# Moving the layer-norm statistics of blocks 8 to 15 into the kernel-generation stage, and splitting two first Fourier stages into halves, in a one-core S4D-plus-GLU kernel

## The chip, the cores and the metric

The kernel runs on one core of a Trainium2 chip. The metric is the device time of one execution in microseconds. The core's engines are PE (TensorE, matrix multiplies; PEld is its weight load), DVE (VectorE), ACT (ScalarE), POOL (GpSimd) and SP (SyncE, which here only issues DMA transfers). Each engine works through its own instructions in order. DMA transfers are issued from queues on SP, ACT and POOL and carried out by sixteen DMA engines.

## The reference

The input u is one sequence of 2048 tokens with 448 features, all in fp32. It is normalised once, and two branches are computed from the normalised sequence and added to u.

```python
xn = layernorm(u)                                  # per token, over 448 features
# branch A: a diagonal state-space convolution, one kernel K of 2048 taps per feature
dt = exp(log_dt); A = -exp(log_A_real) + 1j * A_imag
C  = (C_real + 1j * C_imag) * dt
K  = 2 * real(sum_n C[d, n] * exp(A[d, n] * dt * l))          # 448 x 256 states x 2048 taps
a  = irfft(rfft(xn, 4096) * rfft(K, 4096), 4096)[:2048] + xn * D_skip
# branch B: a gated linear unit with 1792 hidden features
b  = (sigmoid(xn @ w_gate) * (xn @ w_up)) @ w_down
out = u + a + b
```

## The kernel before

**Blocks.** The 2048 tokens are 16 blocks of 128. A block's normalisation needs two statistics per token (mean and variance), from which `x_scales` works out the scale `ys` and the shift `zs` by three Newton steps on DVE. `x_stats` (L246) is one BN_STATS (L248) and one BN_AGGR (L249) of a block; `x_scales` (L251 to L263) is a dozen tiny DVE instructions for as many blocks as one call names; `x_load` (L242) fetches a group of blocks by four DMAs, one for every 32 partitions.

**Two programs, interleaved.** `conv()` is branch A and `glu()` is branch B. Both are Python generators; a loop at the end of the kernel always advances the one that has done the smaller share of its total, where each `yield` states how much work lies behind it. A tile framework then places the instructions on the engines, guided by priorities (`hp`) and by `issue_after`, which holds an instruction back until another one has been issued.

`conv()` goes through these stages:
- startup: it loads blocks 0 to 7 (acc), some weights and the state-space parameters, then blocks 8 to 15 into two tiles (xe0 and xe1, L1037), normalises and transposes the first blocks (L270, L212), and works out the parameters (`prep`, mostly DVE: L300 to L414). After blocks 0 to 7 the statistics of blocks 8 to 15 are taken (L1063 to L1066). The space of xe0 and xe1 is then used for other tiles, P0/P1 and x1a/x1b. The phases go to DRAM (ph_d).
- `kgen` (from L445): 56 chunks, each building a part of the convolution kernel's spectrum. For a chunk, SP loads phases (ph, L475), PE selects them (tr, L526), ACT takes sines of them (S, L535 to L538), POOL multiplies magnitudes (me and mf, L491 and L503), DVE multiplies both (Et at L589 and L590, Ft at L591), and PE contracts Et with Ft (ko, L603). Each fourth chunk is followed by a first Fourier stage of what was gathered (kp and kq, L553), whose result goes through a tile sk to DRAM.
- `spectra`: the products of the spectra and the way back (sp L891, pv L918, L953).

`glu()` runs the 14 tiles of 128 hidden features twice, once for blocks 0 to 7 (half 0) and once for blocks 8 to 15 (half 1). Fp32 products are made of three products of high and low parts. Per tile and group of 512 tokens there are two groups of eleven gate matmuls (gu, L696), a tanh (th, L704), the product hf (L707), its high and low parts hh and hl (L712, L714), and then the down product (po, L809), added up by DVE in acc (L814). In half 0 each tile's weights are loaded (wraw L629 and L631, rd L637), split (wh L746, wl L750, dh and dl) and, for most tiles, also stored in DRAM (wt_d L753, dt_d L776).

**The cross stage.** The last group of half 0 (tiles 12 and 13) also prepares blocks 8 to 15, in pairs of blocks 8, 10, 12 and 14 (a pair is named by its first block): `pair_load` fetches a pair, `pair_norm` normalises it (L270 and L272), `pair_turn` transposes it (L212), and `pair_first` does its first Fourier stage: eight small matmuls (L281) into four PSUM banks named gu, four ACT copies (L678) and eight DMA stores from ACT's queue (L680). Three short tables say where these steps stand: `mid` (between the two gate groups of a tile and token group), `end` (behind it) and `downs` (in the down products). The pool of gu banks has four, shared by gate groups, po, kq, transposes and `pair_first`.

The tables of the kernel before are

```python
mid = [(pair_norm, 8), None, (pair_first, 8), (pair_first, 10)]
end = [(), ((pair_turn, 8), (pair_norm, 10)), ((pair_turn, 10), (pair_norm, 12)), ((pair_turn, 12), (pair_norm, 14))]
downs = {(0, 0): (pair_first, 12), (0, 1): (pair_turn, 14), (0, 3): (pair_first, 14)}
```

## Time and profile before

| what | value |
|---|---|
| median of three runs | 748.35 us (746.88 to 749.01) |
| the profiled execution | 751.69 us |
| its span, first to last instruction | 749.9 us |
| mean granted TensorE clock | 0.981 |
| PE busy | 701.9 us, 94% |
| DVE busy | 558.9 us, 75% |
| ACT and POOL busy | 425.6 us (57%) and 348.2 us (46%) |

The profiled execution has its own time, 751.69 us; its span is 1.8 us shorter, since something lies around the first and last instruction. Durations are read from that execution. A row such as `L603 PE MATMUL ko<-Et,Ft ... [1.54 <-DVE Et L589]` is an instruction of line 603 on PE that writes tile ko from tiles Et and Ft, and before which PE was idle for 1.54 us until DVE's Et of line 589 was there. "x12" stands for twelve in a row. The granted clock is the share of TensorE's full speed that the chip allowed in that stretch.

### The profile page before, as it was taken

The numbers are of one execution on the slowest core, as the hardware profiler recorded it, in microseconds if no ns is written. First come the engines' busy times: TensorE is split into PE (matmuls) and PEld (weight loads), VectorE is DVE, ScalarE is ACT, GpSimd is POOL, SyncE is SP. The second block draws the span as 40 slices with busy tenths as digits, with TensorE's granted clock in tenths as the row PEclk, the third lists the DMA queues.
The fourth block names the chain that finished last, engine by engine and source line by source line (L and its number), as shares of the span: only waits on it lengthen the run. The fifth ranks groups of instructions, "written<-read, shape, count | busy, mean of one in ns | idle before, by whom it ended". The sixth has DMA issues, their size and how long they took to land.

```text
span 749.9 us, 19404 instructions
## 1 busy us (share of the span) xinstructions
PE 701.9 (94%) x7892; PEld 551.8 (74%) x7892; DVE 558.9 (75%) x776; ACT 425.6 (57%) x651; POOL 348.2 (46%) x423
## 2 busy tenths in 40 slices
PE   3997988999999899899999999999999999998995
PEld 2765766887877687666788887887877777776784
DVE  5889996689979789868677978877974555555533
ACT  3553853588677868797676787687743222313320
POOL 2110064785956855846554586387755001351002
PEclk9999998999999999999999999999999999999998
DMA  9965347253225443456942331232158999999845
GB/s 206 232 183 145 87 129 220 62 188 127 72 67 165 127 135 92 136 178 163 278 132 68 109 92 67 91 97 68 42 159 229 268 239 238 236 282 232 198 120 161
DMA packets 98952, 114.75 MB, mean 153 GB/s; under 512 B 11888, under 2 KB 86832, under 8 KB 98864
## 3 DMA queue, kind: packets, MB, share of 16 engines
q1 hardware_dynamic: 74704, 89.11, 43.8%
q10 hardware_dynamic: 21584, 18.24, 8.9%
q0 software_dynamic: 2576, 6.17, 3.2%
q8 instruction: 62, 1.02, 0.6%
q14 instruction: 26, 0.21, 0.1%
HBM read 69.64 MB, written 43.84 MB: 151 GB/s over the span
## 4 chain that ended last, share of the span: by engine, by line
PE 64%; DVE 11%; DMA 8%; ACT 5%; POOL 4%; issue 3%; SPq 3%; ACTq 0%; DVEq 0%; POOLq 0%
PE gu L696 23%; PE po L809 14%; PE sp L891 7%; PE tr L526 7%; PE ko L603 6%; PE pv L918 4%; POOL me L503 2%; PE kp L553 1%; DVE Ft L591 1%; DMA xe<-in_A_u_dram 1%; POOL mf L503 1%; DMA sx<-x_d 1%; DMA ph<-ph_d 1%; DMA wraw<-in_B_w_gate_dram 1%; DVE wl L750 1%
## 5 line engine op out<-in xcount | busy, mean ns | idle before, releaser
L503 POOL TENSOR_TENSOR me<-me,pm 128x32 f32<-128x32 f32 (+1 forms) x168 | 135.1, 804 | 136.2 <-DVE Et L590 125.5
L503 POOL TENSOR_TENSOR mf<-mf,pm 128x64 f32<-128x64 f32 (+1 forms) x112 | 107.4, 959 | 4.6
L696 PE MATMUL gu<-xh,wh 128*128 128x512 f32 x336 | 100.3, 405 | 5.2 <-DVE hf L707 3.4
L696 PE MATMUL gu<-xh,wl 128*128 128x512 f32 x336 | 96.8, 395 | 0.0
L696 PE MATMUL gu<-xl,wh 128*128 128x512 f32 x336 | 96.6, 393 | 0.0
L589 DVE TENSOR_TENSOR Et<-me,S 128x1024 f32<-128x1024 f32 x56 | 80.1, 1430 | 17.1 <-ACT S L538 16.8
L590 DVE TENSOR_TENSOR Et<-me,S 128x1024 f32<-128x1024 f32 x56 | 76.4, 1364 | 16.5 <-ACT me L516 10.7
L809 PE MATMUL po<-dh,hh 128*128 128x448 f32 x224 | 84.9, 380 | 3.9 <-DVE acc L814 3.3
L809 PE MATMUL po<-dl,hh 128*128 128x448 f32 x224 | 82.6, 369 | 0.0
L809 PE MATMUL po<-dh,hl 128*128 128x448 f32 x224 | 82.3, 369 | 0.1
L591 DVE TENSOR_TENSOR Ft<-mf,S 128x1024 f32<-128x1024 f32 x56 | 77.7, 1387 | 3.3 <-ACT S L538 3.1
L696 PEld LDWEIGHTS gu<-xh,wh 128*128 128x128 f32 x336 | 61.2, 190 | 25.7 <-issue 4.7
L535 ACT ACTIVATE S<-tr 128x1024 f32<-128x1024 f32 x56 | 57.5, 1027 | 35.7 <-PE tr L526 35.5
L707 DVE SCALAR_TENSOR_TENSOR hf<-th,gu 128x512 f32<-128x512 f32 x56 | 38.2, 682 | 49.6 <-PE gu L696 38.4
L696 PEld LDWEIGHTS gu<-xh,wl 128*128 128x128 f32 x336 | 63.9, 190 | 14.3 <-DVE wl L750 0.3
L603 PEld LDWEIGHTS ko<-Et,Ft 128*32 128x32 f32 x3584 | 53.7, 110 | 28.0 <-issue 12.7
L696 PEld LDWEIGHTS gu<-xl,wh 128*128 128x128 f32 x336 | 63.5, 189 | 13.7
L603 PE MATMUL ko<-Et,Ft 128*32 128x64 f32 x3584 | 63.9, 221 | 9.4 <-DVE Ft L591 7.8
L712 ACT CAST hh<-hf 128x512 fp32r<-128x512 f32 x56 | 34.9, 623 | 60.8 <-DVE hf L707 58.3
L526 PE MATMUL tr<-sel,ph 128*128 128x512 f32 x224 | 66.5, 419 | 0.4 <-ACT sk L559 0.2
L704 ACT ACTIVATE th<-gu 128x512 f32<-128x512 f32 x56 | 33.7, 601 | 58.4 <-PE gu L696 45.6
L538 ACT ACTIVATE S<-S,hpi 128x1024 f32<-128x1024 f32 x56 | 65.3, 1165 | 0.0
(199 smaller groups left out, 1321.5 us busy)
## 6 DMA issues: line engine op xcount, KB each, us to landing
sk_d<-sk ACTq DMA_DIRECT2D x14, 512.0 KB
sx<-x_d SPq DMA_DIRECT2D x32, 224.0 KB
skl<-sk_d SPq DMA_DIRECT2D x16, 448.0 KB
vp<-v_d SPq DMA_DIRECT2D x16, 448.0 KB
v_d<-vt SPq DMA_DIRECT2D x62, 112.0 KB
wt_d<-wh SPq DMA_DIRECT2D x9, 512.0 KB
wt_d<-wl SPq DMA_DIRECT2D x9, 512.0 KB
wl<-wt_d SPq DMA_DIRECT2D x9, 512.0 KB
```

The lines of the kernel that those rows point to most:

```text
L503: ins = nc.gpsimd.tensor_tensor(m[:, :, w + a : 2 * w : n], m[:, :, a:w:n], par(base + i).unsqueeze(2).to_broadcast([128, 4 * DC, w // n]) ...
L526: nc.tensor.matmul(ps[:, h], ph[:, cn % 2, 128 * h : 128 * h + 128], sel[:, i], start=(i == 0), stop=(i == 1),)
L535: nc.scalar.activation(rows(cs), pv, AF.Abs)
L538: sins[:] = [nc.scalar.activation(cs, cs, AF.Sin, scale=-TWO_PI, bias=hpi)]
L589: v.tensor_tensor(Et[:, :, :, 32:64], two(me[:, :, 32:64]), S[:, 1::-1], ALU.mult)
L590: v.tensor_tensor(Et[:, :, :, 0:32], two(me[:, :, 0:32]), S[:, 1:3, :, ::-1], ALU.mult)
L591: fts[:] = [v.tensor_tensor(Ft, two(mf), S[:, 3:5], ALU.mult)]
L603: mm = nc.tensor.matmul(ko[32 * j : 32 * j + 32, sl], Ft[:, cc, DC * h + 4 * q + j], Et[:, cc, DC * h + 4 * q + j], start=(k == 0), stop=( ...
L696: glu_mm[:] = [nc.tensor.matmul(ps, a_, b_, start=(n == 0), stop=(n == len(mm) - 1))]
L707: marks[1] = v.scalar_tensor_tensor(hf, th, 1.0, pgu[1], ALU.add, ALU.mult)
L809: glu_mm[:] = [nc.tensor.matmul(po, a_[:, bs], w_, start=(n == 0), stop=(n == 3 * fc - 1))]
L891: mm = nc.tensor.matmul(to, tb[:kk, t, 64 * c : 64 * c + 64], rhs, start=True, stop=True, skip_group_check=True,)
```

## The change

It has two parts.

The statistics of blocks 8 to 15 are no longer taken in the startup. The two tiles xe0 and xe1 and their eight loads go; P0/P1 and x1a/x1b get tiles of their own, of the same sizes. Instead, in `kgen`, at the place of the former `yield 34` ahead of the first chunk, four rounds each load a pair of blocks (four DMAs of 32 x 896) into the first part of tile sk and take its statistics, with a yield of 34/4 behind each; the scales of all eight blocks are worked out at the end. All four rounds use the same buffer, so that a round's loads wait until DVE has read the round before.

`pair_first` is generalised to `pair_part(b, xns, gs)`, which does only the groups gs. For the pairs 8 and 10 groups 0 and 1 (`pair_low`, two banks) stay at the place of `pair_first`, and groups 2 and 3 (`pair_high`) move to the end of the third and the fourth step of the cross stage. The pairs 12 and 14 keep all four groups in one place.

```diff
@@ kgen
-        yield 34
+
+        xe = tl["sk"].rearrange("p k e -> p (k e)")[:, : 2 * D].rearrange("p (b d) -> p b d", b=2)
+        for b in range(8, 16, 2):
+            x_load(xe, b, 2, [nc.sync])
+            for i in range(2):
+                x_stats(sm, b + i, xe[:, i])
+            yield 34 / 4
+        x_scales(sm, 8, 8)
@@ pair_first
-    def pair_first(b, xns):
+    def pair_part(b, xns, gs):
-        x1 = pg.tile([128, 2, D], F32, name="x1", tag="wraw", bufs=1)
-        pss = [psg.tile([128, 512], F32, name="gu", bufs=4) for _ in range(4)]
-        for g in range(4):
-            x_first_stage(pss[g][:, :D], xns, g)
-        for g in range(4):
+        x1 = pg.tile([128, 2, D], F32, name="x1", tag="wraw", bufs=1) if 0 in gs else None
+        pss = [psg.tile([128, 512], F32, name="gu", bufs=4) for _ in gs]
+        for ps, g in zip(pss, gs):
+            x_first_stage(ps[:, :D], xns, g)
+        for ps, g in zip(pss, gs):
             to = x1[:, g] if g < 2 else pg.tile([128, D], F32, name="x1", tag="rd", bufs=RB)
-            nc.scalar.copy(to, pss[g][:, :D])
+            nc.scalar.copy(to, ps[:, :D])
             for i in range(2):
                 nc.scalar.dma_start(x1_d[:, row(b + i, g)], to[64 * i : 64 * i + 64])
+    pair_first, pair_low, pair_high = (functools.partial(pair_part, gs=gs) for gs in (range(4), (0, 1), (2, 3)))
@@ glu, cross
-                    mid = [(pair_norm, 8), None, (pair_first, 8), (pair_first, 10)]
-                    end = [(), ((pair_turn, 8), (pair_norm, 10)), ((pair_turn, 10), (pair_norm, 12)), ((pair_turn, 12), (pair_norm, 14))]
+                    mid = [(pair_norm, 8), None, (pair_low, 8), (pair_low, 10)]
+                    end = [(), ((pair_turn, 8), (pair_norm, 10)), ((pair_turn, 10), (pair_norm, 12), (pair_high, 8)), ((pair_turn, 12), (pair_norm, 14), (pair_high, 10))]
@@ conv, startup
-("P2", [CP, 2, 2 * N], F32R), ("xe0", [128, 2048], F32), ("xn0", [128, 4, D], F32), ("xe1", [128, 4, D], F32),
+("P2", [CP, 2, 2 * N], F32R), ("p01", [CP, 2, 2, 2 * N], F32R), ("xn0", [128, 4, D], F32), ("x1ab", [128, 2, 2, D], F32),
-                for q in range(2):
-                    x_load(xes[q], 8 + 4 * q, 4, [nc.sync])
-                with tc.issue_after(xls[0].ins):
-                    for b in range(8):
-                        x_stats(sm, 8 + b, xes[b // 4][:, b % 4])
-                x_scales(sm, 8, 8)
```

The lines of the changed kernel stand seven further down from L573 on, and ten further down behind `pair_part`, so that L589, L603, L696 and L707 of before are its L596, L610, L706 and L717.

The order in which the framework places the instructions changes at three places. The first is DVE's startup, between the Fourier copies of the first blocks (xr, L225) and the parameter work. Before, it read

```order
L225 TENSOR_TENSOR xr<-gu,xr 64x512
L248 BN_STATS st_84<-xe_116 128x6 x4
L300 TENSOR_SCALAR ex<-ex,lim 112x514 x2
L707 SCALAR_TENSOR_TENSOR hf<-th,gu 128x512
L248 BN_STATS st_84<-xe_118 128x6 x4
L249 BN_AGGR mv<-st_84 128x2 x5
L714 TENSOR_TENSOR hl<-hf,hh 128x512
L249 BN_AGGR mv<-st_84 128x2 x3
L750 TENSOR_TENSOR wl<-wraw,wh 128x1024
L707 SCALAR_TENSOR_TENSOR hf<-th,gu 128x512
L256 TENSOR_SCALAR ve<-mv 128x8
```

and now it reads

```order
L225 TENSOR_TENSOR xr<-gu,xr 64x512
L300 TENSOR_SCALAR ex<-ex,lim 112x514 x2
L717 SCALAR_TENSOR_TENSOR hf<-th,gu 128x512
L724 TENSOR_TENSOR hl<-hf,hh 128x512
L717 SCALAR_TENSOR_TENSOR hf<-th,gu 128x512
L760 TENSOR_TENSOR wl<-wraw,wh 128x1024
L724 TENSOR_TENSOR hl<-hf,hh 128x512
L717 SCALAR_TENSOR_TENSOR hf<-th,gu 128x512
L306 SCALAR_TENSOR_TENSOR fr<-ki,ex 112x514 x2
```

All statistics are gone from there, and L306 of the parameter work follows the third hf. On DVE the statistics now stand among the first chunks of `kgen`; the second to the fourth round read

```order
L598 TENSOR_TENSOR Ft<-mf_1054,S_1053 128x1024
L248 BN_STATS st_84<-sk 128x6 x2
L824 SCALAR_TENSOR_TENSOR acc<-po,acc 128x448
L249 BN_AGGR mv<-st_84 128x2 x2
L717 SCALAR_TENSOR_TENSOR hf<-th,gu 128x512
L724 TENSOR_TENSOR hl<-hf,hh 128x512
L248 BN_STATS st_84<-sk 128x6 x2
L249 BN_AGGR mv<-st_84 128x2 x2
L596 TENSOR_TENSOR Et_1050<-me_1055,S_1049 128x32x32
L597 TENSOR_TENSOR Et_1050<-me_1055,S_1049 128x32x32
L598 TENSOR_TENSOR Ft<-mf_1054,S_1049 128x1024
L248 BN_STATS st_84<-sk 128x6 x2
```

The first Ft here belongs to the first chunk, the second Ft to the second, and behind the last BN_STATS come an hf, a wl and the scales, mixed with the Et and Ft of the next chunks.

The second place is SP's queue at the first phase loads. Before, it held

```order
L475 DMA ph_1095<-ph_d 8x2x256 x6
L475 DMA ph_1096<-ph_d 8x2x256 x6
L753 DMA wt_d<-wh 128x1024
L753 DMA wt_d<-wl 128x1024
L629 DMA wraw<-in_B_w_gate_dram 128x3x128
L631 DMA wraw<-in_B_w_gate_dram 64x128 x2
L629 DMA wraw<-in_B_w_up_dram 128x3x128
L631 DMA wraw<-in_B_w_up_dram 64x128 x2
L776 DMA dt_d<-dh 128x448
L776 DMA dt_d<-dl 128x448
L637 DMA rd<-in_B_w_down_dram 128x448
L475 DMA ph_1095<-ph_d 8x2x256 x6
```

and from the first wraw on it now holds (with two sk loads ahead of the first ph and two ahead of wt_d)

```order
L636 DMA wraw<-in_B_w_gate_dram 128x3x128
L638 DMA wraw<-in_B_w_gate_dram 64x128 x2
L244 DMA sk<-in_A_u_dram 32x896 x4
L636 DMA wraw<-in_B_w_up_dram 128x3x128
L638 DMA wraw<-in_B_w_up_dram 64x128 x2
L244 DMA sk<-in_A_u_dram 32x896 x4
L786 DMA dt_d<-dh 128x448
L786 DMA dt_d<-dl 128x448
L475 DMA ph_1057<-ph_d 8x2x256 x4
L244 DMA sk<-in_A_u_dram 32x896 x4
L475 DMA ph_1057<-ph_d 8x2x256 x2
```

Each group of four sk loads of these rows waits for DVE's statistics of the round before; the last stands between the fourth and the fifth of six phase loads.

The third place is PE's order at the first `pair_first` of the cross stage. Before, it read

```order
L526 MATMUL tr<-sel,ph_1096 128x512 x4
L281 MATMUL gu<-xt,wx 64x448 x6
L603 MATMUL ko<-Et_1089,Ft 32x64 x32
L281 MATMUL gu<-xt,wx 64x448 x2
L696 MATMUL gu<-xh,wh 128x512 x3
L696 MATMUL gu<-xr,wh 128x512
L696 MATMUL gu<-xh,wl 128x512 x3
L696 MATMUL gu<-xr,wl 128x512
L696 MATMUL gu<-xl,wh 128x512 x3
L553 MATMUL kp<-wk,ks 64x64 x5
```

and now it reads

```order
L526 MATMUL tr<-sel,ph_1058 128x512 x4
L281 MATMUL gu<-xt,wx 64x448 x4
L706 MATMUL gu<-xh,wh 128x512 x3
L706 MATMUL gu<-xr,wh 128x512
L706 MATMUL gu<-xh,wl 128x512 x3
L706 MATMUL gu<-xr,wl 128x512
L706 MATMUL gu<-xl,wh 128x512 x3
L553 MATMUL kp<-wk,ks 64x64 x7
L610 MATMUL ko<-Et_1051,Ft 32x64 x32
```

The gate group of eleven moved ahead of the chunk's ko, and half of the eight L281 stands later, around the next chunk's ko. Between 165 us and the cross stage, and behind it, the engines' orders are the same before and after but for a few neighbouring loads.

11 lines of the change are left out of this document (4 added, 7 removed).

## The prediction

> **What bounds the kernel now.** I began with the head of the page and its busy line.
>
> ```profile
> span 749.9 us, 19404 instructions
> PE 701.9 (94%) x7892; PEld 551.8 (74%) x7892; DVE 558.9 (75%) x776; ACT 425.6 (57%) x651; POOL 348.2 (46%) x423
> ```
>
> PE is the bound on average, so an engine that is not PE matters only where PE waits for it. Next I asked for the busy time by stretches, because 94% is an average over stages. The columns are the stretch, its length, then busy time (and instructions) of PE, weight load, DVE, ACT and POOL, then granted clock, share of the DMA engines and GB/s.
>
> ```profile
> 28.00:41.30 13.30, 13.30 (x63) 10.10 (x62) 10.25 (x25) 8.79 (x15) 1.13 (x1) 1.00 0.90 196
> 41.30:55.00 13.70, 13.70 (x67) 9.47 (x66) 13.53 (x33) 5.91 (x10) 1.86 (x1) 1.00 0.64 189
> 55.00:112.00 57.00, 49.87 (x237) 36.98 (x236) 56.42 (x87) 32.42 (x53) 13.26 (x7) 0.97 0.43 122
> 131.00:165.00 34.00, 33.98 (x329) 28.06 (x329) 24.55 (x25) 22.95 (x32) 27.39 (x33) 1.00 0.34 109
> 152.00:165.00 13.00, 12.98 (x176) 10.37 (x175) 10.58 (x9) 10.27 (x15) 10.63 (x11) 1.00 0.53 173
> 165.00:187.00 22.00, 20.91 (x229) 17.13 (x227) 20.13 (x27) 17.59 (x26) 13.00 (x15) 1.00 0.44 148
> 600.00:680.00 80.00, 76.98 (x626) 58.86 (x626) 43.37 (x85) 21.31 (x42) 20.40 (x25) 1.00 1.07 253
> ```
>
> Three things are to be seen. From 55 to 112 us DVE is busy 56.42 of 57 us and PE only 49.87: there DVE sets the pace, and DVE work taken away ahead of it should come straight off the time. From 131 to 165 PE is full and DVE has 34 − 24.55 = 9.45 us free. From 600 to 680 the DMA engines are full; that stage's transfers follow from what is computed before them, so I take it to move as a block with what lies ahead.
>
> The chain of waits shows what the startup hangs on (start, duration, what):
>
> ```profile
> 16.82 4.61 DMA ex<-in_A_log_A_real_dram
> 21.45 7.98 DMA xe<-in_A_u_dram
> 29.52 7.32 DMA wraw<-in_B_w_gate_dram
> ```
>
> The loads of the second blocks (xe) are themselves a link of 7.98 us, with a weight load behind them.
>
> **Part 1, the statistics leave the startup.** What goes from DVE is the eight-block statistics. These groups of DVE between 28 and 55 us hold all of it:
>
> ```profile
> L248 DVE BATCH_NORM_STATS2 st<-xe 128x6 f32<-128x448 f32 x8 | 4.4, 615 | 1.3 <-DMA xe<-in_A_u_dram 1.2
> L259 DVE TENSOR_TENSOR z<-ys 128x8 f32<-128x8 f32 x3 | 1.5, 495 | 0.0
> L249 DVE BATCH_NORM_AGGREGATE mv<-st 128x2 f32<-128x6 f32 x8 | 0.7, 155 | 0.0
> L260 DVE SCALAR_TENSOR_TENSOR z<-z,ve 128x8 f32<-128x8 f32 x3 | 0.5, 163 | 0.1
> L261 DVE SCALAR_TENSOR_TENSOR ys<-z,ys 128x8 f32<-128x8 f32 x3 | 0.5, 159 | 0.0
> L257 DVE TENSOR_SCALAR ys<-ve 128x8 int32<-128x8 int32 x1 | 0.2, 172 | 0.0
> L256 DVE TENSOR_SCALAR ve<-mv 128x8 f32<-128x8 f32 x1 | 0.2, 165 | 0.0
> L263 DVE SCALAR_TENSOR_TENSOR zs<-mv,ys 128x8 f32<-128x8 f32 x1 | 0.1, 150 | 0.0
> ```
>
> The sum is 4.4 + 0.7 = 5.1 us for the blocks and 1.5 + 0.5 + 0.5 + 0.2 + 0.2 + 0.1 = 3.0 us for the scales: 8.1 us of DVE. One could also hope for the 7.98 us of loads. Neither comes off whole, because the first 55 us are not DVE's: PE is busy 13.30 of 13.30 and 13.70 of 13.70 us there, and DVE waits for gate results. These two DVE rows are the place where the parameter work (L306) can begin:
>
> ```profile
> 41.33 0.68 DVE L707 SCALAR_TENSOR_TENSOR hf<-th,gu 128x512 f32<-128x512 f32 x1
> 44.30 0.69 DVE L306 SCALAR_TENSOR_TENSOR fr<-ki,ex 112x514 f32<-112x514 int32 x1
> ```
>
> In the new order L306 no longer has scale instructions ahead of it, and its inputs come earlier, but PE still paces the hf rows. I let L306 start at about 41.3, where the hf of 41.33 stands now: 44.30 − 41.3 = 3.0 us gained. Half of the scales' 3.0 us stands behind L306, among parameter work that runs without a pause: another 1.5. So DVE reaches its full stretch **4.5 us** earlier. The ends: 1.5 us if PE holds L306 where it is, and 8.1 us if every removed instruction counted.
>
> **Part 1, what it gives back.** The same 8.1 us come back behind 128 us, in four rounds through one buffer, with 16 loads on SP's queue instead of 8. By the sum they fit into DVE's 9.45 free microseconds, and PE, which is full there, would hide them. Two places do not fit. The first loads stand ahead of the first ph loads:
>
> ```profile
> 122.29 5.22 SPq L475 DMA_DIRECT2D ph<-ph_d x12
> 123.70 1.71 DMA ph<-ph_d
> 148.71 1.99 SPq L475 DMA_DIRECT2D ph<-ph_d x6
> ```
>
> An issue takes 5.22 / 12 = 0.43 us, so two of them delay ph by 0.9 us; ph is on the chain (second row), but ACT's and DVE's weight work ends next to it, so I count half, 0.4. The last round's loads stand behind four of the six ph loads of 148.71: they are issued from 148.71 + 4 × 0.33 = 150.0 to about 151.7 and land at 151.7 + 1.7 = 153.4 by the second row. DVE stands at that round behind the Ft of
>
> ```profile
> 147.63 1.23 DVE L589 TENSOR_TENSOR Et<-me,S 128x1024 f32<-128x1024 f32 x1 [1.76 <-ACT S L538]
> 149.91 1.22 DVE L591 TENSOR_TENSOR Ft<-mf,S 128x1024 f32<-128x1024 f32 x1
> ```
>
> which ends at 151.1. So DVE, which runs in order, waits 2.3 us there; behind the waiting BN_STATS stand an hf, a weight split and the Et and Ft of the next chunks, for which PE's ko waits. Then come a round's statistics, 5.1 / 4 = 1.3, and the scales, 3.0: together 6.6 us, against 13 − 10.58 = 2.4 free from 152 to 165 and 22 − 20.13 = 1.9 from 165 to 187. The overflow is 6.6 − 4.3 = 2.3, less what the earlier arrival of DVE's other work leaves free; with the 0.4 of ph and that relief I book **2.5 us**, between nothing (all of it hidden) and the 8.1 us with the 2.3 us of waiting, 10.4 (nothing hidden). It is nearer to the low end, because the rows show room for most of it. Net of part 1: −4.5 + 2.5 = **−2.0 us**.
>
> The three later rounds also add waits on SP: each load group waits until DVE has read the buffer. What is queued behind are weight loads for later tiles, the stores dt_d, and the two last ph loads; SP has a pause there, from 133.2 to 141.4 us, so I book no more for it:
>
> ```profile
> 132.59 0.59 SPq L631 DMA_DIRECT2D wraw<-in_B_w_up_dram  x1
> 141.41 0.34 SPq L776 DMA_DIRECT2D dt_d<-dh  x1
> ```
>
> **Part 2, halves of two banks.** The rows of the cross stage, PE and DVE mixed:
>
> ```profile
> 301.83 0.85 PE L696 MATMUL gu<-xh,wh 128*128 128x512 f32 x3
> 304.43 0.64 PE L603 MATMUL ko<-Et,Ft 128*32 128x64 f32 x28
> 307.69 0.99 PE L281 MATMUL gu<-xt,wx 32*64 32x448 f32 x12
> 308.84 1.32 DVE L589 TENSOR_TENSOR Et<-me,S 128x1024 f32<-128x1024 f32 x1
> 310.22 1.10 PE L603 MATMUL ko<-Et,Ft 128*32 128x64 f32 x64 [1.54 <-DVE Et L589]
> 312.15 1.60 PE L696 MATMUL gu<-xh,wh 128*128 128x512 f32 x3
> 315.18 1.21 DVE L591 TENSOR_TENSOR Ft<-mf,S 128x1024 f32<-128x1024 f32 x1
> 316.46 0.38 PE L553 MATMUL kp<-wk,ks 64*64 64x64 f32 x5
> 320.25 0.63 PE L603 MATMUL ko<-Et,Ft 128*32 128x64 f32 x26
> 312.20:315.60 3.40, 3.40 (x10) 2.72 (x9) 3.40 (x3) 0.88 (x2) 2.18 (x2) 0.50 0.78 170
> ```
>
> After L281, PE waits 1.54 us for Et, and two microseconds later its clock is granted at 0.50 for 3.4 us (last row). A gate group of eleven matmuls took 304.43 − 301.83 = 2.60 us before, and 316.46 − 312.15 = 4.31 us in that window: 1.71 us lost. In the new order the gate group needs only two banks' worth of L281 ahead of it and stands where PE now waits; ko comes behind it, when Et (done at 310.16) is there: 307.69 + 0.9 + 2.6 = 311.2. No matmul is removed, the other half of L281 comes later. So the wait of 1.54 goes, and the slow window with it: 3.25 us. What is late next is the following ko: its Ft ends at 316.4 and it starts at 320.25, so a PE 3.25 us earlier would ask at 317.0, barely after. The new pieces of L281 need banks and copies at a new place, which no row shows; I keep **−2.5 us**, between −3.3 and +1.0 (a wait as long as the shorter half of the one that goes).
>
> [...]
>
> **The sum** is made against the profiled execution, 751.69 us (span 749.9 and 1.8 around it), which is 3.34 above the median of 748.35: −2.0 − 2.5 = −4.5, to 747.2, and by the median **743.8 us**.
>
> **The rivals.**
>
> *A: only one part works.* A1, the cross stage keeps its loss: another wait replaces the Et wait, for DVE is busy from 308.84 almost without pause and the next Ft is close. Then 748.35 − 2.0 = 746.3. A2, the window of low clock comes anyway, since it could hang on something other than that gap: part 2 gives 1.54 less what I took off, about 1.0, and the time is 748.35 − 2.0 − 1.0 = 745.3. [...] A3, the startup gives all back in the later stretch: 748.35 − 2.5 = 745.9.
>
> *B: the startup was never DVE's.* PE is full to 55 us and holds the gate rows; L306 moves by nothing, 1.5 us come from the scales, 2.5 are given back, and only part 2 remains with a new wait, −1.0: 748.35 + 1.0 − 1.0 = 748.4. Against it: DVE is at 56.42 of 57 from 55 on.
>
> *C: slower.* The one buffer makes a round trip of every later round: DVE must read it, SP then issues four loads (4 × 0.43 = 1.7) and they land 1.7 later, 3.4 us for each of three rounds, if DVE reaches the statistics before the data. DVE being in order, it waits: 8.1 + 10.2 = 18.3 us against 9.45 + 1.9 free, 7.0 over. With −4.5 of the startup and a cross stage that gives nothing that is +2.5: 750.9. It turns the sign from 11.35 + 4.5 − 8.1 = 7.8 us of waiting on, more than two of the three trips. Against it: between two rounds stand Et, Et and Ft (from 147.63 to 151.1, 3.5 us) and gate work, as long as a trip.
>
> **How the numbers follow.** My forecast as worked out 0.44; A1 0.10; A2 0.09; A3 0.11; B 0.09; C 0.17. A measurement of this kernel tells about 0.3%, 2.2 us, from no change: faster is below 746.1, slower above 750.6. The forecast's own range is 740.5 (4.5 + 3.3 from 748.35) to 746. Of the forecast nearly all (0.42), of A2 all but a little and of A3 half are faster, with a rest of A1: 0.58. B, half of A1 and A3 and a piece of C are the same: 0.24. The rest is slower: 0.18. The range for eight in ten goes from 739.5 to 752.0: it holds every case's centre with its nearer bounds, and leaves out the upper part of C and, below, a gain of both parts at their best ends.
>
> **What would show it.** Right: in the new trace no xe link in the chain, L306 near 41, the DVE stretch ending near 107.5 instead of 112; a wait of DVE for sk of some 2 us at the fourth round and none over 1 us at the second and third; ko without a wait at the gate group of the cross stage, and no window at 0.50 there. Wrong: L306 still at 44; waits for sk at several BN_STATS and longer waits of ko for Et or Ft up to 190 us; a new gap before the second half of L281, or a low clock in the cross stage without a gap.

## The result, and the profile after

The changed kernel takes **749.0 us** (median of 22 executions), beside 748.67 us for the kernel before (22 executions on the same chip): a ratio of 1.0007, with a 95% interval from 0.9989 to 1.0026. That is no change. One of the 22 executions of the changed kernel took 790.09 us at a granted clock of 0.846 and is left out of the ratio. A second series gave 749.72 us and 1.0017 (0.9990 to 1.0043). The profiled execution took 748.14 us, with a mean granted clock of 0.984; its page begins

```profile
span 746.3 us, 19407 instructions
PE 701.7 (94%) x7892; PEld 551.7 (74%) x7892; DVE 559.7 (75%) x776; ACT 425.0 (57%) x651; POOL 349.5 (47%) x423
```

PE does the same work as before (701.7 against 701.9 us). Do not read the shorter span (746.3 against 749.9) as a gain: two more profiles of the kernel before, taken during the experiments, had spans of 746.0 and 744.2 us. The first one lost 3 us between 665 and 690 us that neither of these lost. One profile against one profile says nothing here about 3 us. From the Ft of the last chunk to the end the three profiles of before take 194.9, 191.4 and 192.4 us, and two of the changed kernel 192.0 and 195.0.

The stretches of the prediction, in the same columns (length, busy time of PE, weight load, DVE, ACT and POOL, granted clock, share of the DMA engines, GB/s):

```profile
28.00:41.30 13.30, 13.30 (x63) 10.22 (x62) 7.42 (x12) 9.68 (x17) 1.15 (x1) 1.00 0.30 88
41.30:55.00 13.70, 13.70 (x70) 9.88 (x68) 13.70 (x24) 5.17 (x8) 3.49 (x1) 1.00 0.65 205
55.00:112.00 57.00, 47.78 (x222) 34.97 (x220) 52.06 (x80) 31.39 (x51) 14.49 (x7) 0.93 0.38 107
131.00:165.00 34.00, 34.00 (x329) 27.99 (x328) 29.36 (x47) 21.70 (x30) 22.36 (x28) 1.00 0.50 155
165.00:187.00 22.00, 19.63 (x221) 15.49 (x219) 20.12 (x27) 16.61 (x25) 12.80 (x15) 1.00 0.40 136
```

The third row holds the surprise. From 55 to 112 us DVE was busy 56.42 of 57 us; now it is busy 52.06, and PE, which was to run ahead, is busy less than before (47.78 against 49.87 us). DVE has time there and nobody has used it. The fourth row holds the returned statistics: 29.36 − 24.55 = 4.8 us more of DVE, PE full as before. From 165 to 187 us PE is 1.28 us less busy than before (19.63 against 20.91).

I follow the lead that the change gives by three instructions of DVE that exist in every kernel: the fifth and the tenth hf, and the Ft of chunk 5 of `kgen`. In the profile before they stand at

```profile
52.93 0.67 DVE L707 SCALAR_TENSOR_TENSOR hf<-th,gu 128x512 f32<-128x512 f32 x1
114.36 0.67 DVE L707 SCALAR_TENSOR_TENSOR hf<-th,gu 128x512 f32<-128x512 f32 x1
186.67 1.43 DVE L591 TENSOR_TENSOR Ft<-mf,S 128x1024 f32<-128x1024 f32 x1
```

and after, with the first parameter instruction (L306) ahead of them, at

```profile
40.88 1.29 DVE L306 SCALAR_TENSOR_TENSOR fr<-ki,ex 112x514 f32<-112x514 int32 x2
47.59 0.68 DVE L717 SCALAR_TENSOR_TENSOR hf<-th,gu 128x512 f32<-128x512 f32 x1
113.58 0.68 DVE L717 SCALAR_TENSOR_TENSOR hf<-th,gu 128x512 f32<-128x512 f32 x1
187.09 1.43 DVE L598 TENSOR_TENSOR Ft<-mf,S 128x1024 f32<-128x1024 f32 x1
```

So 5.34 us ahead at 53 us, 0.78 ahead at 114, and 0.42 behind at 187. The startup gave its gain, and it was gone before the cross stage. The granted clock, 0.93 instead of 0.97 in the third row, does not explain it: from 53 to 110 us the first profile of before had half clock for 3.4 us and the kernel after for 6.8, but the two other profiles of before had it for 13.7 us and fell back by only 0.9 us between the fifth and the tenth hf, where the kernel after lost 4.56.

**Where it went first: SP's queue.** DVE's waits between 55 and 112 us in the kernel after (what waits, for whom, total, times, longest):

```profile
DVE wl L760 <- ACT wh L756: 3.3, 1, 3.3
DVE w L371 <- ACT junk L360: 1.0, 1, 1.0
DVE w L371 <- ACT w L358: 0.6, 1, 0.6
```

In the first profile of before, DVE waits there once, 0.6 us (1.3 and 1.4 us in the two others). The last two rows are ACT, 1.6 us late in the parameter work where DVE is now early. The first is the weights of tile 6, late on every engine in turn. POOL, ACT, DVE and PE of the kernel after, mixed:

```profile
95.44 7.21 POOL L783 TENSOR_TENSOR dl<-rd,dh 128x448 fp32r<-128x448 f32 x1 [7.35 <-ACT dh L782]
110.12 1.04 ACT L756 CAST wh<-wraw 128x1024 fp32r<-128x1024 f32 x1 [7.76 <-DMA ph_d<-p]
111.20 1.23 DVE L760 TENSOR_TENSOR wl<-wraw,wh 128x1024 fp32r<-128x1024 f32 x1 [3.34 <-ACT wh L756]
112.24 1.22 PE L706 MATMUL gu<-xh,wh 128*128 128x512 f32 x2 [4.72 <-ACT th L714]
116.73 1.14 POOL L783 TENSOR_TENSOR dl<-rd,dh 128x448 fp32r<-128x448 f32 x1
```

The weight split wh waited 7.76 us for its data (the wait is put down to a store that had long been issued; by its place it is the load of wraw). SP's queue tells why. Before, with POOL's dl of tile 4 (two loads of wraw, then rd):

```profile
98.08 7.68 POOL L773 TENSOR_TENSOR dl<-rd,dh 128x448 fp32r<-128x448 f32 x1 [8.69 <-ACT dh L772]
95.76 0.38 SPq L629 DMA_DIRECT2D wraw<-in_B_w_gate_dram  x1
97.87 0.59 SPq L629 DMA_DIRECT2D wraw<-in_B_w_up_dram  x1
105.79 0.35 SPq L637 DMA_DIRECT2D rd<-in_B_w_down_dram  x1
```

and after (rd first, then wraw):

```profile
93.91 2.82 SPq L389 DMA_DIRECT2D ph_d<-p  x2
102.68 0.35 SPq L644 DMA_DIRECT2D rd<-in_B_w_down_dram  x1
103.14 0.40 SPq L636 DMA_DIRECT2D wraw<-in_B_w_gate_dram  x1
105.90 0.49 SPq L636 DMA_DIRECT2D wraw<-in_B_w_up_dram  x1
```

SP issues here in the order of its queue, rd at 102.68 and the wraw behind it at 103.14. rd has two buffers, so tile 6's rd waits for POOL's dl of tile 4, which ends at 95.44 + 7.21 = 102.65, and rd is issued at 102.68. The wraw loads behind it leave at 103.14 instead of 95.76, 7.4 us later. Before, the same dl was as slow (7.68 us, to 105.76) and rd waited for it in the same way (105.79), but the wraw loads had already gone. So it is the order in the queue that changed, not the dl. The other profiles of the change repeat the order; PE's wait there is 2.7 to 3.1 us instead of 4.72 (c1, e1 and e1b of the table below).

What stands beside the slow dl shows in the rows as well. Another dl takes 1.14 us at 116.73. While the slow one runs, DVE runs ten two-input instructions without a pause, from 95.02 to 101.58, and dl ends 1.0 us after the last of them; while the fast one runs, DVE waits. So one subtraction of 128x448 took 7.21 us beside a DVE without a pause and 1.14 beside a waiting one. That DVE's work holds POOL up there is my reading of these rows; how it would do so they do not show.

**The returned statistics.** DVE of the kernel after, at the last round and the scales, and (last row) the last round in a second profile of the same kernel, c1:

```profile
150.04 1.16 DVE L248 BATCH_NORM_STATS2 st<-sk 128x6 f32<-128x448 f32 x2 [0.68 <-DMA sk<-in_A_u_dram]
153.59 0.93 DVE L257 TENSOR_SCALAR ys<-ve 128x8 int32<-128x8 int32 x1
156.15 1.02 DVE L260 SCALAR_TENSOR_TENSOR z<-z,ve 128x8 f32<-128x8 f32 x1
157.70 1.11 DVE L261 SCALAR_TENSOR_TENSOR ys<-z,ys 128x8 f32<-128x8 f32 x1
161.87 0.17 DVE L261 SCALAR_TENSOR_TENSOR ys<-z,ys 128x8 f32<-128x8 f32 x1
151.33 1.15 DVE L248 BATCH_NORM_STATS2 st<-sk 128x6 f32<-128x448 f32 x2 [2.23 <-DMA sk<-in_A_u_dram]
```

In the first profile 0.68 us is the only wait for sk of all four rounds. That belongs to this execution: c1 waits 2.23 us at the fourth round and 0.91 at the third, and the two profiles of part 1 alone (e1 and e1b below) 2.03 and 2.40 at the fourth and 0.6 at the third. The scales come on top. Of the twelve tiny scale instructions eleven took 0.15 to 0.17 us each before, and one, beside POOL, 1.16 us. After, four of them take 0.55 to 1.11 us beside POOL's work: twelve take 4.93 us instead of 3.0 (3.83 in c1, e1 and e1b). The row at 161.87 shows the same instruction at 0.17 us in a moment without POOL.

**The cross stage.** PE of the kernel after, where it waited 1.54 us before:

```profile
308.02 0.98 PE L281 MATMUL gu<-xt,wx 32*64 32x448 f32 x8
308.93 0.96 PE L706 MATMUL gu<-xh,wh 128*128 128x512 f32 x3
312.24 1.10 PE L610 MATMUL ko<-Et,Ft 128*32 128x64 f32 x64
316.54 0.97 PE L281 MATMUL gu<-xt,wx 32*64 32x448 f32 x4
317.90 0.96 PE L281 MATMUL gu<-xt,wx 32*64 32x448 f32 x2
319.13 0.96 PE L281 MATMUL gu<-xt,wx 32*64 32x448 f32 x2
341.58 0.87 PE L610 MATMUL ko<-Et,Ft 128*32 128x64 f32 x46 [0.82 <-DVE Et L596]
```

The gate group stands ahead of ko and ko finds its Et: the wait is gone, and in this execution the clock stays at 1.00. What is paid: the second half of the eight (eight records, as the first) comes in three pieces. Two records take 0.96 us, four 0.97, eight 0.98, so three pieces cost almost three times one. And a wait of 0.82 us for Et stands at 341.58. With whole pairs the same sixteen records come in two pieces, here in e1b:

```profile
307.07 0.99 PE L281 MATMUL gu<-xt,wx 32*64 32x448 f32 x12
310.64 0.97 PE L281 MATMUL gu<-xt,wx 32*64 32x448 f32 x4
```

The sum can be made over the cross stage, from 298 to 352 us, in profiles whose clock stays at 1.00 there. With whole pairs (c2, e1, e1b) L281 comes in nine pieces of 8.9 to 9.0 us together, and PE's waits add up to 3.3 to 3.5 us. With halves (after, e2, e9, e11) it is eleven pieces of 10.7 us and 1.6 to 1.9 us of waits. The halves save about 1.6 us of waiting and pay about 1.8 us in pieces.

### The profile page after: what moved, and what is told of

Same layout as the page of the kernel before. It is cut to its first block, busy times and chain, and to the rows that moved or that the text cites. A ratio compares the mean times of both kernels' runs of the same rounds, so it can differ in the third digit from the quotient of the medians.

```text
span 746.3 us, 19407 instructions
## 1 busy us (share of the span) xinstructions
PE 701.7 (94%) x7892; PEld 551.7 (74%) x7892; DVE 559.7 (75%) x776; ACT 425.0 (57%) x651; POOL 349.5 (47%) x423
## 3 DMA queue, kind: packets, MB, share of 16 engines
q8 instruction: 62, 1.02, 0.6%
## 4 chain that ended last, share of the span: by engine, by line
PE 44%; DMA 5%; DVE 2%; ACT 1%; issue 0%; ACTq 0%; SPq 0%; POOL 0%; POOLq 0%; DVEq 0%
PE gu L706 16%; PE po L819 9%; PE sp L901 6%; PE tr L526 4%; PE ko L610 3%; PE pv L928 3%; DMA sk_d<-sk 1%; DMA tb<-in_c_tab_dram 1%; DMA sx<-x_d 1%; PE kp L553 1%; DMA t<-in_c_t_dram 1%; DMA out_dram<-ac 1%; PE kq L553 1%; PE pv L963 0%; DVE yy L915 0%
## 5 line engine op out<-in xcount | busy, mean ns | idle before, releaser
L503 POOL TENSOR_TENSOR mf<-mf,pm 128x64 f32<-128x64 f32 (+1 forms) x112 | 107.5, 960 | 4.4
L706 PE MATMUL gu<-xh,wh 128*128 128x512 f32 x336 | 99.9, 403 | 6.5 <-ACT th L714 5.4
L706 PE MATMUL gu<-xl,wh 128*128 128x512 f32 x336 | 97.0, 393 | 0.0
L706 PE MATMUL gu<-xh,wl 128*128 128x512 f32 x336 | 95.8, 392 | 0.0
L596 DVE TENSOR_TENSOR Et<-me,S 128x1024 f32<-128x1024 f32 x56 | 79.8, 1425 | 11.2 <-ACT S L538 11.1
L597 DVE TENSOR_TENSOR Et<-me,S 128x1024 f32<-128x1024 f32 x56 | 75.1, 1341 | 17.0 <-ACT me L516 11.2
L706 PEld LDWEIGHTS gu<-xh,wh 128*128 128x128 f32 x336 | 60.9, 189 | 27.4 <-ACT th L714 6.3
L706 PEld LDWEIGHTS gu<-xh,wl 128*128 128x128 f32 x336 | 63.5, 189 | 14.1
L610 PEld LDWEIGHTS ko<-Et,Ft 128*32 128x32 f32 x3584 | 54.0, 110 | 26.5 <-issue 12.9
L706 PEld LDWEIGHTS gu<-xl,wh 128*128 128x128 f32 x336 | 63.2, 189 | 13.4
L717 DVE SCALAR_TENSOR_TENSOR hf<-th,gu 128x512 f32<-128x512 f32 x56 | 38.2, 682 | 46.1 <-PE gu L706 37.2
L610 PE MATMUL ko<-Et,Ft 128*32 128x64 f32 x3584 | 64.1, 222 | 8.5 <-DVE Ft L598 7.6
L824 DVE SCALAR_TENSOR_TENSOR acc<-po,acc 128x448 f32<-128x448 f32 x80 | 48.1, 613 | 23.7 <-PE po L819 23.7
```

The source lines that it names most:

```text
L503: ins = nc.gpsimd.tensor_tensor(m[:, :, w + a : 2 * w : n], m[:, :, a:w:n], par(base + i).unsqueeze(2).to_broadcast([128, 4 * DC, w // n]) ...
L596: v.tensor_tensor(Et[:, :, :, 32:64], two(me[:, :, 32:64]), S[:, 1::-1], ALU.mult)
L597: v.tensor_tensor(Et[:, :, :, 0:32], two(me[:, :, 0:32]), S[:, 1:3, :, ::-1], ALU.mult)
L610: mm = nc.tensor.matmul(ko[32 * j : 32 * j + 32, sl], Ft[:, cc, DC * h + 4 * q + j], Et[:, cc, DC * h + 4 * q + j], start=(k == 0), stop=( ...
L706: glu_mm[:] = [nc.tensor.matmul(ps, a_, b_, start=(n == 0), stop=(n == len(mm) - 1))]
L824: v.scalar_tensor_tensor(acc[:, b], po, 0.5, acc[:, b], ALU.mult, ALU.add)
```

## The experiments

Every time is the median of 11 or 12 executions, every ratio is to the kernel before on the same chip, with its 95% interval. The edits are against the changed kernel unless stated. Since whole times scatter by some microseconds, the table also gives, for each profile, the start of the same DVE instruction less its start in the first profile of before (52.93, 114.36, 186.67), and how much that difference changes from chunk 21 to chunk 34, from 302 to 409 us, around the cross stage. "low" is the length of a stretch at half clock in the cross stage, a window in what follows. e10, described below, is not in the table.

| run | 5th hf | 10th hf | Ft, chunk 5 | 302 to 409 us | low, us |
|---|---|---|---|---|---|
| before | 0 | 0 | 0 | 0 | 3.4 |
| before again (c0) | −0.05 | +0.88 | −0.50 | −0.03 | 3.4 |
| before again (c2) | −1.23 | −0.29 | −1.41 | −1.53 | none |
| after | −5.34 | −0.78 | +0.42 | −0.91 | none |
| after again (c1) | −4.65 | −0.24 | +0.46 | +1.44 | 6.8 |
| part 1 alone (e1) | −4.85 | −0.35 | +0.17 | −1.54 | none |
| part 1 alone again (e1b) | −4.82 | −0.72 | +0.10 | −1.50 | none |
| part 2 alone (e2) | +0.79 | +0.99 | −0.65 | −1.71 | none |
| weights of tile 6 early (e3) | −4.61 | −1.30 | −0.71 | +0.74 | 3.4 |
| no statistics (e4) | −4.80 | −0.20 | −1.32 | −1.92 | none |
| no statistics, weights early (e5) | −4.85 | −2.62 | −3.08 | +1.02 | 6.8 |
| e3 and dl of tile 4 on DVE (e6) | −5.09 | −3.02 | −1.03 | −1.91 | none |
| second halves late (e7) | −5.11 | −0.56 | +0.10 | +2.65 | none |
| first loads past SP (e8) | −4.71 | −2.64 | +3.87 | −2.28 | none |
| scales late (e9) | −4.87 | −0.53 | −0.59 | −1.71 | none |
| e6 and scales late (e11) | −4.91 | −1.75 | −1.14 | −1.39 | none |

**The two parts alone.** Part 1 alone keeps whole pairs in the tables of the cross stage:

```diff
-mid = [(pair_norm, 8), None, (pair_low, 8), (pair_low, 10)]
+mid = [(pair_norm, 8), None, (pair_first, 8), (pair_first, 10)]
-end = [..., (pair_norm, 12), (pair_high, 8)), (..., (pair_norm, 14), (pair_high, 10))]
+end = [..., (pair_norm, 12)), (..., (pair_norm, 14))]
```

> Part 1 alone: the statistics are moved, the first Fourier stages of all four pairs stay whole. Theory S (the startup's gain of some 4 us is lost twice, first on SP's queue, where the weights of tile 6 now stand behind a rd load and ph_d stores, then to the scales among chunks 2 and 3): up to the cross stage this run is like the changed kernel, Ft of chunk 20 at +0.3 us against before, gap of about 4.7 us near 107, and the cross stage like before, so the time is that of before plus 0.3 us, ratio 1.000. Rival R (the startup keeps its 2 us and it is the cross stage that loses them): Ft of chunk 20 at about -2 us and a ratio of 0.997.

> Part 1 alone, a second time, on another set of executions. If part 1 alone is really slower than the changed kernel: ratio 1.003 to 1.005 again, with a loss that its second profile shows, most likely the half-clock window behind the 1.5 us wait near 309, which its first profile did not have. If the first ratio (1.0038, from 1.0006 to 1.0069) was high by chance: 1.000 to 1.002.

It took 751.25 us, 1.0038 (1.0006 to 1.0069), and in a second series 748.77 us, 1.0023 (0.9994 to 1.0052). Part 1 brings nothing; if anything it costs 0.2 to 0.4%. By the table it stands at chunk 5 where the kernel after stands (within 0.3 us), 0.1 to 0.2 behind the first profile of before.

Part 2 alone is the kernel before with the halves (the old startup statistics, `yield 34` in `kgen`).

> Part 2 alone, on the kernel before. If the cross stage behaves as in the changed kernel: nothing differs up to 305 us, the wait for Et of 1.54 us and the half clock behind it are gone, chunk 24 starts about 3.5 us earlier, and by chunk 33 only 0.9 us are left, so the time is 0.9 us below before, ratio 0.999. If the loss behind the cross stage belonged to part 1: 3 us stay, ratio 0.996.

It took 747.62 us, 0.9999 (0.9975 to 1.0022): nothing to be seen.

**The clock window without its wait, and the wait without its window.** The second profile of the changed kernel has no edit:

> The changed kernel once more, with a profile of its own, to see what of its first profile repeats. If the account so far is the kernel's: the startup's lead of about 5 us at the fifth hf is down to 1 us or less at the ninth, wh of tile 6 waits 7 to 8 us and is cast at 110 us, Ft of chunk 5 stands at +0.4 against before within 0.6, PE's loss in the cross stage (296 to 350 us) is 9.2 us, and the ratio is 0.999 to 1.002. If those belong to one execution: other places and other losses.

Its rows, where PE does the pieces of L281 and just behind:

```profile
317.20:320.60 3.40, 3.40 (x34) 1.08 (x32) 1.80 (x3) 3.35 (x6) 3.24 (x7) 1.00 0.77 236
320.60:327.40 6.80, 6.80 (x56) 5.10 (x55) 4.38 (x5) 3.53 (x7) 3.22 (x5) 0.50 0.25 56
```

Half clock for 6.8 us, with no wait of PE over 0.1 us in the 13 us ahead. The profile of part 1 alone (e1b) is the counterpart:

```profile
309.61 1.10 PE L610 MATMUL ko<-Et,Ft 128*32 128x64 f32 x64 [1.54 <-DVE Et L596]
309.00:312.00 3.00, 2.40 (x70) 1.56 (x71) 1.87 (x3) 2.93 (x6) 2.84 (x4) 1.00 0.28 66
312.00:316.00 4.00, 4.00 (x59) 3.06 (x57) 4.00 (x4) 1.10 (x2) 2.76 (x3) 1.00 0.86 195
```

The very same wait of 1.54 us, and no window. All five profiles with whole pairs have the wait, two of them (before, c0) a window. Of the ten with halves at the places of the change three have one (c1, e3, e5). So the wait is neither needed for the window nor enough for it. Brief idling of PE does not stand ahead of it either: in the row ahead of c1's window PE is busy 3.40 of 3.40 us and only weight load is light, 1.08 us. The kernel after has such a row without a window behind it:

```profile
316.40:319.80 3.40, 3.40 (x33) 1.08 (x32) 1.65 (x3) 3.34 (x6) 3.24 (x7) 1.00 0.74 222
```

What differs is where these rows lie. In every trace the clock changes only on a grid: each stretch between two changes, but for the last of the trace, is a whole number of steps of 3.413 us (in the first profile of before 15, 1, 13, 2, 20, 1, 18, 1, 16, 1, 107, 1 and 18 steps). Where the grid falls against the kernel's work differs between executions: an edge stands at 319.1 us in the kernel after, in c1 at 317.2 and 320.6. In c1, e3 and e5 the light stretch, the pieces of L281 (from 316.54 us in the kernel after), fills one step (weight load 1.02 to 1.08 us in it) and half clock begins with the next. In the seven other profiles with halves an edge of the grid cuts that stretch, at 319.1 us in the row above, and its lightest step has 1.27 to 1.85 us of weight load. So within these ten the window goes with the place of the grid, which would explain why one kernel has it in one execution and not in the next. What a step must hold stays open: with whole pairs, steps with 1.21 and 1.13 us of weight load (before, c0) were followed by half clock, and steps with 1.00, 0.94 and 1.19 (c2, e1b, e1) were not.

Two profiles of the kernel before complete the count:

> The kernel before, profiled once more, to see how far two profiles of one kernel agree place by place. If the differences between the profiles read so far are the kernels': Ft of chunks 0, 5, 20 and 40 within 0.3 us of the first profile. If part of them is the run's own (arrival of the startup's loads, windows of half clock): differences of 0.5 to 2 us, and the half-clock windows at other places, above all with or without the one behind the 1.54 us wait near 309 us.

> The kernel before, profiled a third time, to count its half-clock windows in the cross stage. If the window hangs on the wait of 1.5 us and the place in the fixed grid of 3.4 us: the wait is there again, the window perhaps not (it was there in two profiles of the kernel before, and not in the one of part 1 alone with the same wait). Ft of chunks 5 and 20 within 0.7 us of the first profile.

They took 747.8 and 746.01 us (one execution each). At chunk 5 the three profiles of before differ by 1.4 us, from 302 to 409 us by 1.5 us with and without window.

**Both second halves late (e7).**

```diff
-end = [..., (pair_norm, 12), (pair_high, 8)), (..., (pair_norm, 14), (pair_high, 10))]
+end = [..., (pair_norm, 12)), (..., (pair_norm, 14), (pair_high, 8), (pair_high, 10))]
```

> The changed kernel with the second halves of both pairs at the end of the fourth step, so that L281 of pair 8 is not scattered among the ko of chunk 24. If the saving of the cross stage (the wait of 1.54 us) is eaten by the scattered pieces, 0.66 us for two L281 against 0.43 for four: PE's loss against its own pace from 296 to 350 us is some 0.8 us below the 9.2 of the changed kernel; ratio to before 0.999. If the deferred work costs wherever it stands: the loss stays at 9 to 10 us, with a wait at another place.

753.38 us, 1.0062 (1.0039 to 1.0084), the clearest loss of all, and +2.65 from 302 to 409 us. Two rows of PE and one of ACT:

```profile
339.51 1.19 PE L526 MATMUL tr<-sel,ph 128*128 128x512 f32 x4 [2.42 <-ACT S L537]
345.17 0.47 PE L819 MATMUL po<-dh,hh 128*128 128x448 f32 x1 [1.47 <-ACT x L686]
344.58 0.53 ACT L686 COPY x<-gu 128x448 f32<-128x448 f32 x1 [2.79 <-DMA x_d<-x]
```

PE waits for ACT's sines and for a copy, 3.9 us. The last of the four copies (L686) of the second halves, now at one place, itself waits 2.79 us for a store from the buffers it shares, of which there are two. That the crowding of the copies also makes the sines late is argued, not shown. The place of the second halves matters more than the wait that the halving removes.

**Where the startup's lead goes: statistics or queue?** e4 leaves out the rounds and the scales of blocks 8 to 15 and sets ys and zs to constants:

```diff
+    nc.gpsimd.memset(ys[:, 8:16], 20.0)
+    nc.gpsimd.memset(zs[:, 8:16], 0.0)
...
-        for b in range(8, 16, 2):
...
-        x_scales(sm, 8, 8)
+        yield 34
```

> The changed kernel without the statistics of blocks 8 to 15 at all: their loads, BN_STATS, BN_AGGR and scales are left out, and two constants stand for the scales, so blocks 8 to 15 are normalised by constants. Theory S: Ft of chunk 0 as in the changed kernel, about -2 us against before, and chunks 2 and 3 keep it (-1.8 instead of +2.0 and +0.4); time 2 us below the changed kernel, ratio 0.997. Rival (another chain, POOL's magnitudes or the phase loads, holds chunks 3 to 5): Ft of chunk 5 still at +0.4 us, ratio 1.000.

747.09 us, 0.9997 (0.9968 to 1.0026). Without any statistics at all the kernel is no faster than before. The lead of 4.80 at the fifth hf is down to 0.20 at the tenth, where no statistics have come back yet in any kernel. So the first loss is not the returned work. The expectation, a ratio of 0.997, was not met. e3 is the kernel after with tile 6's weights ahead in SP's order and its rd on another queue; e5 is the same on top of e4:

```diff
-  raw, rd = raws.pop() if raws else (w_load(f), None)
+  with hp(HP) if f == 6 else nullcontext():
+      raw, rd = raws.pop() if raws else (w_load(f), None)
...
-  rd = rd or rd_load(f)
+  rd = rd or rd_load(f, eng=nc.gpsimd if f == 6 else nc.sync)
```

> The changed kernel, with the weight load of tile 6 given priority and its rd load taken from POOL's queue, so that on SP the six weight loads stand ahead of the ph_d stores that wait for POOL. Theory S: wh of tile 6 is cast at about 104 us instead of 110, the gap of 4.7 us near 107 is gone or below 1 us, the first Ft comes about 3 us earlier than in the changed kernel (near 134.5 us), and what the scales then take leaves Ft of chunk 3 some 2 us earlier; time 746 to 747, ratio 0.997. Rival (the parameter work itself is late, the weights only wait beside it): the gap may go, but Ft of chunks 0 and 3 stay within 0.5 us, ratio 1.000.

> The changed kernel without the statistics of blocks 8 to 15 (loads, BN_STATS, BN_AGGR and scales left out, constants in place of the scales), and with the weights of tile 6 ahead of the ph_d stores on SP. If SP's order at tile 6 is what ate the startup's gain: the phase loads are issued near 118 us instead of 121.7, Ft of chunk 0 at -4 us against before and Ft of chunk 5 at -3; ratio 0.994. If the parameter work behind 55 us (DVE with POOL, to the last ph_d store) is the limit: phase loads near 121, Ft of chunk 0 at -3 at most and of chunk 5 at -1.5 to -2, ratio 0.997.

750.02 us, 1.0034 (1.0009 to 1.0059), and 747.67 us, 0.9982 (0.9959 to 1.0005). In e5 the loads, the split and the gate group stand at

```profile
97.96 0.40 SPq L632 DMA_DIRECT2D wraw<-in_B_w_gate_dram  x1
103.04 1.05 ACT L753 CAST wh<-wraw 128x1024 fp32r<-128x1024 f32 x1 [0.18 <-DMA wraw<-in_B_w_up_dram]
112.47 1.65 PE L702 MATMUL gu<-xh,wh 128*128 128x512 f32 x3 [2.18 <-DVE hf L713]
```

The load leaves 5.2 us earlier than in the kernel after, the split is 7.1 us earlier. At chunk 5 e5 is 1.76 ahead of e4, e3 1.15 ahead of the two profiles of the kernel after: the queue's order costs 1.2 to 1.8 us. The statistics cost 0.44 + 1.32 = 1.76 (after against e4) and 3.08 − 0.71 = 2.37 (e3 against e5). These are differences of single profiles: at chunk 5 the five profiles with part 1's startup as it stands (after, c1, e1, e1b, e7) lie within 0.4 us, the three of before within 1.4. Even e5, with neither loss, keeps 2.62 of its 4.85 at the tenth hf. The whole time of e3 does not show its 1.15; its profile has a window in the cross stage.

**More of the lead (e6), and the round trip (e8).** e6 adds to e3 the dl of tile 4 on DVE instead of POOL; e8 adds to e6 the first round's loads on ACT's queue and the rd of tile 7 on POOL's.

```diff
-  nc.gpsimd.tensor_tensor(dl, rd, dh, ALU.subtract)
+  (v if f == 4 else nc.gpsimd).tensor_tensor(dl, rd, dh, ALU.subtract)
... e8:
-  x_load(xe, b, 2, [nc.sync])
+  x_load(xe, b, 2, [nc.scalar if b == 8 else nc.sync])
...
-  rd = rd or rd_load(f, eng=nc.gpsimd if f == 6 else nc.sync)
+  rd = rd or rd_load(f, eng=nc.gpsimd if f in (6, 7) else nc.sync)
```

> The changed kernel with the weights of tile 6 ahead on SP, and the subtraction dl of tile 4, which took 7.2 us on POOL beside a busy DVE, on DVE instead (some 0.6 us there). If POOL's long dl holds the parameter stores (its six L393 follow it): L393 begins near 96 us instead of 104, the phase loads are issued at 118 to 119 us, Ft of chunk 0 at -4.5 us and of chunk 5 at -2.5; ratio 0.996. If DVE is the limit (POOL's last L393 wait for L401 and L403 in any case): phase loads within 1 us of 122, Ft of chunk 5 at -0.7 us, ratio 1.000 to 1.003 as without it.

> The kernel with the weights of tile 6 ahead and dl of tile 4 on DVE, and besides with less on SP ahead of the first phase loads: the rd load of tile 7 on POOL's queue, the first four sk loads on ACT's. If SP's queue holds the phase loads (in the run before, the last ph_d store was issued at 116.3 us and the first ph load at 121.4, with a weight load, rd and two sk loads between): ph at 119 to 119.5 us, Ft of chunk 0 at -5 us against before and of chunk 5 at -2.5; ratio 0.997. If the weights of tile 7 pace the stage anyway: ph earlier, but Ft of chunk 5 at -1 as without it; ratio 1.000.

e6: 748.65 us, 0.9997 (0.9968 to 1.0025); at the tenth hf it is 3.02 ahead, at chunk 5 1.03. e8: 751.5 us, 1.0051 (1.0021 to 1.0082). It brings the slower rival to life. DVE's waits between 125 and 175 us:

```profile
DVE st L248 <- DMA sk<-in_A_u_dram: 10.1, 2, 8.3
```

With the first round early, SP holds the next rounds behind phase loads and DVE, in order, waits 10.1 us for sk; chunk 5 is 3.87 late, 4.9 worse than e6.

**The scales later (e9, e10, e11).**

```diff
-        x_scales(sm, 8, 8)
...
+        if cn == 9:
+            with tc.issue_after(fts[0].ins):
+                x_scales(sm, 8, 8)
```

> The changed kernel with the twelve small scale instructions held back to chunk 9, where DVE waits 2.5 us for a gate result; the BN_STATS stay. If the scales among chunks 2 and 3 (0.5 to 1.1 us each beside POOL, instead of 0.17) are what the statistics cost: Ft of chunk 2 at -1 instead of +2.0 us and of chunk 5 at -1; ratio 0.998. If it is the loads and the fourth round's wait: Ft of chunk 5 stays at 0 to +0.4.

> Everything that helped in one kernel: the startup's lead kept (weights of tile 6 and phase loads ahead, dl of tile 4 on DVE), and the scales held back to chunk 9. By the sum of the parts Ft of chunk 5 at -3 to -4 us against before, the cross stage at 9.2 us of loss; ratio 0.995. If the parts hide one another: -1.5 to -2 and ratio 0.998.

> The version that the runs point to: the changed kernel with the weights of tile 6 ahead on SP, dl of tile 4 on DVE, and the scales held back to chunk 9, SP's phase loads as in the changed kernel. By the sum of the parts Ft of chunk 5 stands at -2 us against before (-1.0 with the first two, 1.0 more from the scales) and at the end of the convolution at -2 to -4, depending on whether the cross stage meets a half-clock window; ratio 0.996 to 0.999. If the startup's lead does not reach the end at all: ratio 1.000 and more.

e9 (after with this): 749.32 us, 1.0010 (0.9983 to 1.0036); chunk 5 is 1.0 earlier than in the kernel after, whole time the same. e10 (e8 with this): 748.8 us, 1.0014 (0.9984 to 1.0043); its profile, of the longest of its twelve executions, is not used. e11 (e6 with this) joins what had helped: 747.9 us, 0.9999 (0.9976 to 1.0023). At chunk 5 it is 1.14 ahead, not 2 as the sum of the parts said. No version here beats the kernel before beyond the interval.

## Why the prediction was right or wrong

**Startup: the lead was right, its worth was not.** L306 starts at 40.88, forecast about 41.3. The four profiles with part 1 as it stands (after, c1, e1, e1b) are 4.92 ahead at the fifth hf on average, the three of before 0.43: a lead of 4.5 us, as forecast. The step that failed is "DVE work taken away ahead of it should come straight off the time". At the tenth hf the same means leave 0.52 + 0.20 = 0.7 us. A row with DVE at 56.42 of 57 shows that DVE was last before; it does not show how far behind it the next ones were. They were close: ACT's parameter work (1.6 us of new waits), then tile 6's weights, whose loads moved behind a blocked rd in SP's queue (wait of 4.72 on PE). e5, e6 and e8, without the second, have 2.8 to 3.2 left against the mean of before (+0.20), which is about 4.5 − 1.6; but e3, with the same edit as e5, has only 1.5, and e11, with the startup of e6, only 1.9. That the difference is ACT's 1.6 fits the best of them in size, but was not tried apart. The prediction listed what SP's queue would have to carry behind 128 us, and never asked what an earlier DVE changes in SP's order ahead of that.

**What part 1 gives back: right in size, and mostly in kind.** Forecast 2.5 us, measured 1.8 to 2.4 (e4, e5, single profiles). The wait for the last round, forecast 2.3 us, is 2.23, 2.03 and 2.40 in three profiles and 0.68 in one. The scales were priced too low: beside POOL they take 3.8 to 4.9, not 3.0 us, and moving them (e9) recovers about 1.0. The two loads ahead of the first phase load hold SP for 0.9 to 2.0 us (forecast 0.9, half of it counted); the phase load is issued at 121.7 to 123.4 us, before at 121.2 to 123.6, so what they cost can't be told from the scatter. Together: part 1 stands at chunk 5 at +0.29 on average, before at −0.64, so it is 0.9 us later instead of 2.0 earlier. As before's three profiles differ by 1.4 us there, the 0.9 may be nothing; the forecast lead of 2.0 is not there.

**Cross stage: the wait went, the window did not hang on it.** The failed step is "So the wait of 1.54 goes, and the slow window with it: 3.25 us". The first half of it holds in every profile with halves, and the following ko is not late, as forecast. The second half rested on one row of one execution. Taking only profiles without a window, halves stand at −1.69 from 302 to 409 us (seven: after, e2, e4, e6, e8, e9, e11), whole pairs at −1.52 (three: c2, e1, e1b): the halving is worth 0.2 us, which is less than the scatter among the seven (−0.91 to −2.29). The 1.54 is spent: the prediction took 0.75 us off 3.25 for "the new pieces of L281", and they cost about 1.8 us more than the whole, against 1.6 us of waits saved over the stage, which cancel within the scatter. A window itself costs 1.5 us with whole pairs (before and c0 against −1.52), not far from the 1.71 that the prediction read, but halves have windows too. Rival A2, the window hanging on something else, had the right thought, but took 1.0 for what is left. By that thought part 2 is worth the wait alone, 1.54 us at most, the better number, and c1 speaks for it: 6.8 us at half clock with no wait of PE over 0.1 us ahead.

**The rivals.** The result lies inside the range for eight in ten, but that range was wide enough to hold no change, and the forecast was a gain of 4.5 us. B's time, 748.4, lies nearest to the result, but that is luck: its mechanism is not what happened, L306 did move. C's mechanism, DVE waiting for round trips of one buffer, occurs in the change only in small, 0.7 to 3.1 us of waits in all, and in full in e8, with 10.1 us of waits and 4.9 us at chunk 5 against e6.

**The signs I had named.** L306 near 41 and ko without a wait came true; the DVE stretch did not end near 107.5, the tenth hf is at 113.58; the wait of some 2 us for sk at the fourth round is there in three of the four profiles of part 1 and 0.68 in the first; the low clock is absent in one profile of the change and present in the other. That the xe link leaves the chain can't be read: the chain of the kernel after breaks off at 360 us.

**Open.** Part 1 alone measures 0.2 to 0.4% slower (1.7 to 2.8 us), of which its profiles show 0.9 us by chunk 5 and no more in the cross stage. Where the rest is, if it is there, was not found: its two series overlap with the result of the whole change, and from the last chunk to the end two profiles of one kernel differ by up to 3.5 us. So the prediction's block that moves along behind 600 us could not be tested at this size, and a lead of a microsecond at chunk 5 can't be followed to the end. Taking POOL's work away from DVE's statistics altogether, or spreading the statistics over other stages, was not tried.

## What to carry to other kernels

An engine that is busy 99% of a stretch is the bound only down to the next one (here 4.5 us of lead became 0.7): before its gain is booked, ask for every engine and queue at that place how far behind it is, DMA queues above all, because a reordered load behind one blocked buffer can cost much of what the change gained (here it left SP 7.4 us later, and the order cost 1.2 to 1.8 us). A low-clock window or a long wait seen in one execution is not yet a property of the kernel (the window stood in two of five profiles with whole pairs): take a second profile of the kernel before, and price only what stands in both. When work is moved beside another engine, price it with durations measured beside that engine (here 3.8 to 4.9 us for the scales beside POOL, not 3.0).

## What was not expected of the hardware

- Half clock came for 6.8 us (0.50 from 320.6 us in c1) with no wait of PE over 0.1 us ahead of it, and stayed away behind a wait of 1.54 us in three of five profiles.
- Tiny DVE instructions (128x8) took up to 1.16 us beside POOL's work (before, at 46.80 us) and 0.17 without; a POOL subtraction of 128x448 took 7.21 us beside a full DVE and 1.14 beside a waiting one.
- The granted clock changed only in whole steps of 3.413 us in every trace, and where this grid fell against the kernel's work differed between executions.
- Two of the small Fourier matmul records (L281) take as long as eight, 0.96 against 0.98 us.
- Three profiles of one kernel differed by 1.4 us at 187 us and had spans of 749.9, 746.0 and 744.2 us.
